# A row scratch with a pitch of 1,280 bytes, in place of a Pool clear between row scatters

## The chip, the cores and the metric

The kernel runs on one core of a Trainium2 chip. The metric is the device time of one execution in microseconds (us), smaller is better; the median of several runs is given with their spread. The engines that matter here are PE (TensorE: matmuls, and PEld, its weight loads), DVE (VectorE), ACT (ScalarE), POOL (GpSimd, which also issues the DMAs of its own queue) and SP (SyncE, which here only issues DMAs). Each engine works through its own instructions in program order and waits on semaphores for the others.

## The reference

Two stages. The first is an attention in which the blocks of k and v are mixed by a Sinkhorn-normalised matrix, with batch 4, 8 heads, 768 positions and head size 64, in 8 blocks of 96 positions. The second is a mixture of 8 experts with one expert per token, on 3,072 tokens of width 512.

```python
for _ in range(5):                      # P: 8 x 8 for each batch and head
    P = np.exp(P - np.max(P, axis=-1, keepdims=True))
    P = P / (np.sum(P, axis=-1, keepdims=True) + 1e-09)
    P = P / (np.sum(P, axis=-2, keepdims=True) + 1e-09)
k_sorted = np.einsum('bhij,bhjcd->bhicd', P, k_b)      # v likewise
attn = softmax(q_b @ k_sorted^T / 8)                   # inside each block of 96
x = (attn @ v_sorted)                                  # 3072 tokens x 512
logits = x @ w_gate + modality_bias[modality_id]
e_idx = np.argmax(logits, axis=1)
gate_w = softmax(logits)[e_idx]
for e in range(8):
    h = np.maximum(x[mask] @ w1[e], 0.0)               # 512 -> 1024
    out[mask] = gate_w[mask, None] * (h @ w2[e])       # 1024 -> 512
```

## The kernel before

**Chunks.** The attention runs in 32 units; unit u is one head of two batches and four blocks. Eight units finish one chunk: 768 tokens in 8 tiles of 96, all 512 columns of them. The four chunks are called m = 0 to 3. A finished chunk lies in SBUF as `xb`, 96 partitions by 8 tiles by 516 bf16 columns: 512 of x, then the token's number and its gate weight as two 32-bit words.

**Routing.** When a chunk is complete, `gate_T` and `gate_L` compute its logits, `choose(m)` takes the expert of each token, and `place(m)` (lines 491 to 544) gives each token a row in a scratch in DRAM. The scratch, `xs_dram` (line 54), has a region of 3,328 rows for each expert, plus 256 rows at its end; a row is 258 32-bit words, 1,032 bytes, and the next row begins right behind it. PE counts ranks into `rk`; DVE turns them into a row number per token: `selr` (L508), `dstf` (L511), and `dest`, the same as integers (L512). The gate weight goes into `xb` at L516, the token's number by a Pool copy at L520. Then `one(t)` (lines 524 to 537) is called for t = 0 to 7: each call sends the 96 rows of one tile to their places with an indirect DMA on Pool's queue (L529). From t = 1 on a `nop` goes before it, and in chunks 1 to 3 also a Pool `memset` of 128 partitions by 512 columns of `kT[0]` (L527), a tile that nothing reads any more by then.

**Slots.** The experts work on slots of 256 rows. `x_fetch` (L650 to L661) reads a slot from the scratch: a DMA transpose (L652) on SP's queue brings x, with its 512 columns on the partitions, into one of four `xT` buffers, and a small DMA (L656) brings the token numbers and gates into `idg`. Of the two experts that get most tokens, `table(m)` (L556) tells after each chunk which slots are full: after chunk 0 slots 0 and 1, after chunk 1 slots 2 and 3, after chunk 2 slots 4 to 7, after chunk 3 slots 8 to 11 and a last half slot 12. The first transpose of each such group waits for all eight scatters of its chunk. `pad_fill` (L622) writes 256 rows of zeros behind the last token of each of the two experts, `zero_block` (L617) does so at the scratch's end; `pair_rows` (L606) is the view of 256 rows that these and L656 use. Whatever is left for other experts is done in a loop at the end, which is empty for this input.

**Experts.** For each slot `mL1` (L681) multiplies with the first weights (4 steps of 8 matmuls into `hp`, L685) and `mL2` (L705) with the second (2 steps of 8 matmuls into `yp`, L708); `y_out` (L689) scales the result by the gate (L695 on ACT or L697 on DVE) and scatters it to the output with an indirect DMA on Pool's queue (L699).

**Order.** The order of the program is written out by hand: the loop over the units (L891 to L903) interleaves scores, softmax and attention of the units with these steps, and from unit 16 on with the experts' steps, one or two for each unit (`pace`, L888). So each engine has one fixed order, in which PE's expert steps of a new group of slots stand among the attention units of the next chunk. Pool's queue holds, one behind the other: the scatters of a chunk with what lies between them, then the output scatters (L699) of the slots that were ready meanwhile, then the token numbers' copy (L520) of the next chunk.

Of the kernel before, what the change touches and what calls it, by code (L numbers as in the profile page):

```python
# [12 lines left out]
ALU = mybir.AluOpType  # L13
# [4 lines left out]
def kernel(  # L18
# [13 lines left out]
    nc = tc.nc  # L32
# [4 lines left out]
    N, Dm = out.shape  # L37
    E = moe_w_gate.shape[1]
    F = moe_w1.shape[2]

    GW = Dm + 4
    NTL = N // BLK
    PR = 256
    CAP = N + PR
    ZR = E * CAP
# [5 lines left out]
    I32 = mybir.dt.int32  # L51
    SYNC = mybir.DependencyInfo(mybir.DependencyClass.Sync, mybir.DependencyReason.DATA)

    xs_dram = nc.dram_tensor("xs_scratch", [ZR + PR, GW // 2], I32, kind="Internal").ap()

    singles = ctx.enter_context(tc.tile_pool(name="singles", bufs=1))
    small = ctx.enter_context(tc.tile_pool(name="small", bufs=1))
# [16 lines left out]
    kT = [singles.tile([128, GC], BF16, tag=f"kT{g}", name=f"kT{g}") for g in range(2)]  # L74
# [4 lines left out]
    attnT = [singles.tile([96, 8 * BLK + 32], BF16, tag=f"attnT{z}", name=f"attnT{z}") for z in range(2)]  # L79
    xb = [singles.tile([BLK, 8, GW], BF16, tag=f"xb{z}", name=f"xb{z}") for z in range(2)]  # L80
    xTg = [singles.tile([128, 8, BLK], BF16, tag=f"xTg{z}", name=f"xTg{z}") for z in range(2)]
# [6 lines left out]
    hT_b = [t.rearrange("p (f r) -> p f r", f=8) for t in (hT_0, qTb[0][:, 4096:6144])]  # L88
    zpad = singles.tile([128, GW], BF16, tag="zpad")

    def q_in(g, hh):
# [8 lines left out]
    nc.sync.dma_start(out=BT[:, 0:2], in_=moe_modality_bias.rearrange("(o m) e -> o m e", o=1).broadcast_to([128, 2, E]))  # L100
    modI = xTg[1].rearrange("p a b -> p (a b)").bitcast(I32)[0:NTL, 0:2 * BLK]
    nc.sync.dma_start(out=modI, in_=bass.AP(tensor=mod_w.tensor, offset=mod_w.offset,
                                            ap=[[2 * BLK, NTL], [1, 2 * BLK]]))
    wg_sb = singles.tile([128, 4, E], FP32)
# [11 lines left out]
    def load_q(g, h0, nh):  # L116
        t = q_in(g, h0 // 4).rearrange("p (r h f) -> p r h f", r=2, h=4)
        z = h0 % 4
        for par in range(2):
            nc.gpsimd.dma_start(out=t[:, par, z:z + nh], in_=q[2 * g + par, h0:h0 + nh]  # L120
                                .rearrange("h (p t) d -> p h (t d)", t=6))
# [8 lines left out]
    pI = singles.tile([128, 1], I32)  # L130
    idI = singles.tile([BLK, NTL], I32)
    load_q(0, 0, 2)
# [9 lines left out]
    nc.gpsimd.iota(pI, pattern=[[0, 1]], base=0, channel_multiplier=1)  # L142
    nc.gpsimd.iota(idI, pattern=[[BLK, NTL]], base=0, channel_multiplier=0)
    nc.gpsimd.iota(jI, pattern=[[1, 2], [0, 2]], base=0, channel_multiplier=0)
# [18 lines left out]
    for e in range(1, E):  # L163
# [7 lines left out]
                     ap=[P_t.ap[0], P_t.ap[2], P_t.ap[1]])  # L171
# [3 lines left out]
                   ap=[ident.ap[0], [1, NB], [NB, 16]])  # L175
# [81 lines left out]
    for it in range(5):  # L257
# [10 lines left out]
        for f in gap[it]:  # L268
# [7 lines left out]
                       ap=[red.ap[0], [0, NB], red.ap[1]])  # L276
# [29 lines left out]

    biasm = singles.tile([BLK, NTL, E], FP32)
    modB = singles.tile([NTL, 6, 16], BF16)
    modF = singles.tile([BLK, NTL], FP32)
# [30 lines left out]
    def use(act=0.0, dve=0.0):  # L340
        busy[0] += act
        busy[1] += dve
# [148 lines left out]
    def place(m):  # L491
        oh, ls = oh_t[m]
        xt = xb[m % 2]
        prev = ohs[m % 2]
        rk = mipsum.tile([128, 8, E], FP32, tag="mi", name=f"rk{m}")
        rkf = rk.rearrange("p t e -> p (t e)")
        pb = bass.AP(tensor=prev.tensor, offset=prev.offset, ap=[prev.ap[0], [0, 8], prev.ap[1]])
        nc.tensor.matmul(rkf, maskUT[0:BLK, :], oh.rearrange("p t e -> p (t e)"), start=True, stop=False,
                         skip_group_check=True)
        nc.tensor.matmul(rkf, ones_bf[0:BLK, :], ebase.rearrange("p t e -> p (t e)"), start=False, stop=False,  # L500
                         skip_group_check=True)
        nc.tensor.matmul(rk, ones_bf[0:BLK, :], pb, start=False, stop=False, skip_group_check=True)
        for t in range(7):
            ob = bass.AP(tensor=oh.tensor, offset=oh[:, t].offset, ap=[oh.ap[0], [0, 7 - t], [1, E]])
            nc.tensor.matmul(rk[:, t + 1:8], ones_bf[0:BLK, :], ob, start=False, stop=(t == 6),
                             skip_group_check=True)
        sel_r = small.tile([BLK, 8, E], FP32, tag="selr", name=f"selr{m}")
        nc.vector.tensor_tensor(sel_r, rk[0:BLK], oh, ALU.mult)  # L508
        dest = small.tile([BLK, 8], I32, tag="dest", name=f"dest{m}")
        dstf = small.tile([BLK, 8], FP32, tag="dstf", name=f"dstf{m}")  # L510
        nc.vector.tensor_reduce(dstf, sel_r, AX.X, ALU.add)  # L511
        nc.vector.tensor_copy(dest, dstf)  # L512
        sm = small.tile([BLK, 8, 1], FP32, tag="sm", name=f"sm{m}")
        nc.vector.tensor_reduce(sm, ls, AX.X, ALU.add)
        gcol = xt.bitcast(FP32)[:, :, Dm // 2 + 1:Dm // 2 + 2]
        nc.vector.reciprocal(gcol, sm)  # L516
        g, hf = m // 2, m % 2
        icol = xt.bitcast(I32)[:, :, Dm // 2]
        idm = idI.rearrange("p (b f j) -> p b f j", b=4, f=2)[:, 2 * g:2 * g + 2, hf]
        nc.gpsimd.tensor_copy(icol.rearrange("p (r j) -> p r j", r=2), idm)  # L520
        scat[m] = []
        use(dve=1.5)

        def one(t):
            if t:
                if m:
                    nc.gpsimd.memset(kT[0][:, 0:512], 0.0)  # L527
                nc.gpsimd.nop()
            ins = nc.gpsimd.indirect_dma_start(  # L529
                out=xs_dram, out_offset=bass.IndirectOffsetOnAxis(ap=dest[:, t:t + 1], axis=0),  # L530
                in_=xt.bitcast(I32)[:, t], in_offset=None)
            after = []
            tc.declare_no_dep(ins.ins, group="xs", reason="rows are disjoint", **({"keep": after} if after else {}))
            tc.add_to_no_dep_group("xs", ins.ins)
            for pre in after:
                tc.add_manual_dep(ins.ins, pre.name, SYNC, reason="rows leave at an even pace")
            scat[m].append(ins.ins)
        ones_[m] = one
        for t in range(8):
            one(t)  # L540
        nxt = ohs[(m + 1) % 2]
        ohsum = small.tile([BLK, E], FP32, tag="ohsum", name=f"ohsum{m}")
        nc.vector.tensor_reduce(ohsum, oh.rearrange("p t e -> p e t"), AX.X, ALU.add)
        nc.vector.tensor_tensor(nxt, ohsum, prev, ALU.add)
# [59 lines left out]
    pads = []  # L604

    def pair_rows(row):  # L606
        return xs_dram[bass.ds(row, PR)].rearrange("(t p) w -> p t w", t=2)

    zsrc = zpad.bitcast(I32)
    zsrc2 = bass.AP(tensor=zsrc.tensor, offset=zsrc.offset, ap=[zsrc.ap[0], [0, 2], zsrc.ap[1]])  # L610

    def in_xs_group(ins, keep=()):
        kw = {"keep": list(keep)} if keep else {}
        tc.declare_no_dep(ins, group="xs", reason="rows are disjoint or ordered by hand", **kw)
        tc.add_to_no_dep_group("xs", ins)

    def zero_block():  # L617
        ins = nc.sync.dma_start(out=xs_dram[ZR:ZR + PR].rearrange("(t p) w -> p t w", t=2), in_=zsrc2)
        in_xs_group(ins.ins)
        pads.append(ins.ins)  # L620

    def pad_fill(e, own=True):  # L622
        row = nc.values_load(prow[0:1, e:e + 1], engines=(SPEng,), min_val=0, max_val=ZR - PR)
        ins = nc.sync.dma_start(out=pair_rows(row), in_=zsrc2)
        if own:
            in_xs_group(ins.ins)
            pads.append(ins.ins)
# [22 lines left out]
    def x_fetch(s, row, own, after=(), n=PR):  # L650
        view = xs_dram[bass.ds(row, n)]
        i1 = nc.sync.dma_start_transpose(out=xT_b[s % NX][:, :, 0:n], in_=view.bitcast(BF16)[:, 0:Dm])  # L652
        xins[s] = i1
        if own:
            nc.sync.nop()
        i2 = nc.sync.dma_start(out=idg_b[s % NI], in_=pair_rows(row)[:, :, Dm // 2:GW // 2])  # L656
        if own:
            for i in (i1, i2):
                in_xs_group(i.ins, after)
                for a in after:  # L660
                    tc.add_manual_dep(i.ins, a.name, SYNC, reason="rows of the slot")  # L661
# [133 lines left out]
    make_upper_triangular(nc, maskUT, val=1.0, diag=False)  # L795
    nc.gpsimd.iota(zpad.bitcast(I32)[:, Dm // 2:Dm // 2 + 1], pattern=[[0, 1]], base=SKIP, channel_multiplier=0)
    zero_block()

    st = {"tab": -1, "x": 0, "l1": 0, "done": 0, "pos": 0}
# [110 lines left out]
    choose(3)  # L910
    run_pieces(2)
    place(3)
    run_pieces(2)
    table_x(3)
# [35 lines left out]
    for s in range(NREST):  # L950
# [3 lines left out]
        row = nc.values_load(tR2[0:1, s:s + 1], engines=(SPEng,), min_val=0, max_val=ZR)  # L954
# [36 lines left out]
```

## Time and profile before

| | |
|---|---|
| median of 3 runs | 214.34 us (212.81, 214.34, 214.37) |
| the profiled execution: its time | 212.81 us |
| its span, first to last instruction | 210.9 us |
| so, around the span | 1.9 us |
| mean clock granted to TensorE | 0.876 of full |
| PE busy | 169.5 us, 80% of the span |
| DVE / ACT / POOL busy | 103.7 / 93.2 / 94.9 us |
| row scatters (L529) | 32 of 0.925 us mean, 29.6 us of POOL |
| clears between them (L527) | 21 of 0.539 us median |
| output scatters (L699) | 25 of 0.982 us mean |
| first to last row scatter of chunks 0, 1, 2, 3 | 54.98 to 64.16, 80.25 to 91.83, 111.68 to 123.07, 142.48 to 153.88 us |

Times are counted from the span's start. A line of the timeline gives the start, the duration, the engine (SPq is SP's queue), the source line and operation, what it writes and reads, how many instructions are merged, and in brackets how long the engine was idle before it and what ended that. In the chain of waits, each line is a start, the time that the step takes on the path that ended last, and what it is. A row of the table of stretches gives a stretch, its length, PE's busy time and number of matmuls in it, the granted clock, the busy share of the 16 DMA engines and the GB/s that they moved.

### The profile page before, as it was taken

Reading aid. Unit: us, or ns where it says so; the run is one execution under the profiler, and the core shown is the slowest. Engines: PE = TensorE matmul, PEld = TensorE weight load, DVE = VectorE, ACT = ScalarE, POOL = GpSimd, SP = SyncE. Lnnn points to the kernel's source line nnn. Section 1 sums busy time; section 2 is a strip of 40 time slices with the busy share of each in tenths; the row PEclk is TensorE's granted clock in tenths of the full one; section 3 lists DMA queues with packets and bytes.
Section 4 is the critical chain, followed back from the end, with each engine's and each line's share of the span. In section 5 each row is a group of like instructions: output and inputs, shape, how many; then the busy total and the mean of one; then the engine's idle time right before and its main releaser. Section 6 shows DMA issues by size and latency. Waiting matters only on the chain.

```text
span 210.9 us, 5167 instructions
## 1 busy us (share of the span) xinstructions
PE 169.5 (80%) x2045; PEld 122.5 (58%) x2045; DVE 103.7 (49%) x333; ACT 93.2 (44%) x148; POOL 94.9 (45%) x139
## 2 busy tenths in 40 slices
PE   6397497769999799995899993999995999999200
PEld 2136496659789686863666753767754667654000
DVE  5968377855787777850355551358221232222100
ACT  2037277836788776853335831334321222232000
POOL 7901378920472027984007983048972232323300
PEclk9859679955699999999559999799999999999955
DMA  4999999999993789729101239536239852212100
GB/s 59 211 225 200 199 223 195 201 181 218 204 242 86 87 131 188 176 82 252 28 0 38 60 106 240 82 83 208 58 105 234 155 99 78 81 71 99 61 2 0
DMA packets 30160, 27.66 MB, mean 131 GB/s; under 512 B 18831, under 2 KB 25775, under 8 KB 29872
## 3 DMA queue, kind: packets, MB, share of 16 engines
q0 software_dynamic: 11792, 23.10, 49.9%
q1 hardware_dynamic: 18336, 4.16, 11.8%
q8 instruction: 18, 0.29, 0.6%
q14 instruction: 14, 0.11, 0.2%
HBM read 27.35 MB, written 10.52 MB: 180 GB/s over the span
## 4 chain that ended last, share of the span: by engine, by line
PE 57%; DVE 10%; POOL 9%; issue 7%; DMA 7%; ACT 4%; POOLq 0%; DVEq 0%; SPq 0%; ACTq 0%
PE hp L685 18%; PE yp L708 16%; DMA xT<-xs_scratch 6%; PE va L375 4%; PE ka L366 3%; PE sc L418 3%; POOL xs_scratch L529 3%; PE gt L450 3%; PE lg L456 3%; DVE xb L441 3%; PE op L437 3%; POOL v_sb L120 2%; PE warm L249 2%; ACT v_sb L353 2%; POOL kT L527 2%
## 5 line engine op out<-in xcount | busy, mean ns | idle before, releaser
L685 PE MATMUL hp<-xT,w 128*128 128x256 bf16 x384 | 51.2, 287 | 8.8 <-DMA xT<-xs_scratch 8.7
L685 PEld LDWEIGHTS <-w 128*128 128x128 bf16 x384 | 37.6, 102 | 18.5 <-DMA xT<-xs_scratch 9.4
L529 POOL DMA_INDIRECT xs_scratch<-xb,dest x32 | 29.6, 925 | 36.6 <-issue 35.3
L699 POOL DMA_INDIRECT out_dram<-kvb,idg x25 | 24.5, 982 | 42.4 <-DVE kvb L697 20.8
L424 ACT ACTIVATE attnT<-sc 96x768 bf16<-96x768 f32 x32 | 25.9, 809 | 13.4 <-PE sc L418 13.0
L708 PE MATMUL yp<-w,hT 128*128 128x512 bf16 x96 | 22.8, 382 | 0.0
L708 PE MATMUL yp<-w,qT 128*128 128x512 bf16 x96 | 22.7, 379 | 0.0
L441 DVE TENSOR_TENSOR xb<-op,rs 96x512 bf16<-96x512 f32 x32 | 22.0, 687 | 1.2
L679 ACT ACTIVATE hT<-hp 128x512 bf16<-128x512 f32 x17 | 10.1, 597 | 22.0 <-PE hp L685 21.8
L697 DVE TENSOR_SCALAR kvb<-yp,idg 128x512 f32<-128x512 f32 x11 | 8.3, 751 | 20.2 <-PE yp L708 20.2
L695 ACT ACTIVATE kvb<-yp,idg 128x512 f32<-128x512 f32 x13 | 8.9, 688 | 17.6 <-PE yp L708 17.6
L679 ACT ACTIVATE qT<-hp 128x512 bf16<-128x512 f32 x16 | 9.6, 597 | 14.7 <-PE hp L685 14.3
L437 PE MATMUL op<-v_sb,attnT 96*128 96x65 bf16 x256 | 14.4, 202 | 0.8 <-DVE xb L441 0.4
L708 PEld LDWEIGHTS <-hT 128*128 128x128 bf16 x96 | 9.1, 99 | 9.3 <-issue 0.3
L708 PEld LDWEIGHTS <-qT 128*128 128x128 bf16 x96 | 9.1, 98 | 9.0
L418 PE MATMUL sc<-qT,kT 64*128 64x96 bf16 (+1 forms) x256 | 12.7, 223 | 1.8 <-ACT attnT L424 0.9
L375 PE MATMUL va<-bd,kvb 128*128 128x128 bf16 x128 | 13.5, 269 | 0.0
L440 DVE RECIPROCAL rs<-op 96x8 f32<-96x8 f32 x32 | 6.4, 199 | 13.7 <-PE op L437 13.7
L437 PEld LDWEIGHTS <-attnT 96*128 96x128 bf16 x256 | 11.8, 103 | 1.9 <-DVE xb L441 0.8
L366 PE MATMUL ka<-bd,kvb 128*64 128x64 bf16 x384 | 9.6, 216 | 4.0 <-issue 2.8
L375 PEld LDWEIGHTS <-kvb 128*128 128x128 bf16 x128 | 12.6, 195 | 0.2
L450 PE MATMUL gt<-ident,xb 96*128 96x96 bf16 x128 | 9.4, 224 | 4.2 <-DVE xb L441 4.1
(180 smaller groups left out, 241.5 us busy)
## 6 DMA issues: line engine op xcount, KB each, us to landing
w<-in_moe_w_dram POOLq DMA_DIRECT2D x4, 1024.0 KB
kvb<-in_k_dram POOLq DMA_DIRECT2D x4, 768.0 KB
kvb<-in_v_dram POOLq DMA_DIRECT2D x2, 1536.0 KB, 17.8
q_in<-in_q_dram POOLq DMA_DIRECT2D x4, 384.0 KB, 16.5
xs_scratch<-zpad SPq DMA_DIRECT2D x3, 258.0 KB
v_sb<-in_q_dram POOLq DMA_DIRECT2D x4, 192.0 KB, 4.0
v_sb<-in_q_dram POOLq DMA_DIRECT2D x2, 384.0 KB, 19.8
xs_scratch<-xb,dest POOLq DMA_INDIRECT x32, 3.3
```

What stands on the lines that cost most here:

```text
L366: nc.tensor.matmul(acc[par * 64:(par + 1) * 64, z], k_raw[:, (c0 + z) * D:(c0 + z + 1) * D], bd[g][:, par * 64:(par + 1) * 64], start=True ...
L375: nc.tensor.matmul(acc[:, z], v_cols[:, d0 + z], bd[g], start=True, stop=True)
L418: nc.tensor.matmul(sc[0:m, par, j * BLK:(j + 1) * BLK], kT[g][rows, x0:x0 + m], qT[rows, i], start=True, stop=True)
L424: mark[0] = nc.scalar.activation(attnT[u % 2][:, 0:8 * BLK].rearrange("p (r f) -> p r f", r=2), sc_tiles.pop(u)[0:BLK, :, 0:4 * BLK], ACT. ...
L437: nc.tensor.matmul(ov[:, par, j], attnT[u % 2][:, c0:c0 + 128], v_sb[g][0:BLK, par * 64 + h * 8 + i, 0:D + 1], start=True, stop=True)
L441: nc.vector.tensor_tensor(xt[:, :, h * D:(h + 1) * D].rearrange("p (r j) d -> p r j d", r=2), ov[0:BLK, :, :, 0:D], rs.broadcast_to([BLK, ...
L450: nc.tensor.transpose(tp[:, t], xb[m % 2][:, t, c * 128:(c + 1) * 128], ident[:BLK, :BLK])
L529: ins = nc.gpsimd.indirect_dma_start(out=xs_dram, out_offset=bass.IndirectOffsetOnAxis(ap=dest[:, t:t + 1], axis=0), in_=xt.bitcast(I32)[: ...
L679: mark[0] = nc.scalar.activation(dst, src, ACT.Relu)
L685: nc.tensor.matmul(hp[:, f], w_at(s, c * F + (2 * j + f) * 128, 128), xT_b[s % NX][:, c], start=(c == 0), stop=(c == 3))
L699: ins = nc.gpsimd.indirect_dma_start(out=out, out_offset=bass.IndirectOffsetOnAxis(ap=idg[:, t, 0:1], axis=0), in_=y, in_offset=None, boun ...
L708: nc.tensor.matmul(yp, hT_b[s % 2][:, fc, t * 128:(t + 1) * 128], w_at(s, 4 * F + fc * Dm, Dm), start=(fc == 0), stop=(fc == 7))
```

## The change

The scratch's rows get a pitch of XP = 5 * 512 / 8 = 320 words, 1,280 bytes (five times 256), of which the first 258 words are used as before. Each row so begins on a multiple of 256 bytes from the scratch's start. The scatter's target is seen as a list of single words, and `dest` holds the word at which the row begins (the row number times 320) in place of the row number. The views that read and fill rows take the first 258 words of each. The `memset` between the scatters of chunks 1 to 3 goes; the `nop` stays.

```diff
     GW = Dm + 4
+    XP = 5 * Dm // 8
...
-    xs_dram = nc.dram_tensor("xs_scratch", [ZR + PR, GW // 2], I32, kind="Internal").ap()
+    xs_dram = nc.dram_tensor("xs_scratch", [ZR + PR, XP], I32, kind="Internal").ap()
...
         nc.vector.tensor_reduce(dstf, sel_r, AX.X, ALU.add)
-        nc.vector.tensor_copy(dest, dstf)
+        nc.vector.tensor_scalar(dest, dstf, float(XP), None, ALU.mult)
...
         def one(t):
             if t:
-                if m:
-                    nc.gpsimd.memset(kT[0][:, 0:512], 0.0)
                 nc.gpsimd.nop()
             ins = nc.gpsimd.indirect_dma_start(
-                out=xs_dram, out_offset=bass.IndirectOffsetOnAxis(ap=dest[:, t:t + 1], axis=0),
+                out=xs_dram.rearrange("r (x o) -> (r x) o", o=1), out_offset=bass.IndirectOffsetOnAxis(ap=dest[:, t:t + 1], axis=0),
                 in_=xt.bitcast(I32)[:, t], in_offset=None)
...
     def pair_rows(row):
-        return xs_dram[bass.ds(row, PR)].rearrange("(t p) w -> p t w", t=2)
+        return xs_dram[bass.ds(row, PR), 0:GW // 2].rearrange("(t p) w -> p t w", t=2)
...
     def zero_block():
-        ins = nc.sync.dma_start(out=xs_dram[ZR:ZR + PR].rearrange("(t p) w -> p t w", t=2), in_=zsrc2)
+        ins = nc.sync.dma_start(out=xs_dram[ZR:ZR + PR, 0:GW // 2].rearrange("(t p) w -> p t w", t=2), in_=zsrc2)
```

## The prediction

> **What bounds the kernel now.** I read the page's slices first, to find where PE isn't full and where its clock is low.
>
> ```profile
> PE   6397497769999799995899993999995999999200
> ...
> PEclk9859679955699999999559999799999999999955
> ```
>
> A slice is 5.27 us. From slice 11 on PE is nearly full except at slices 18, 24 and 30 (about 95, 126 and 158 us), and the granted clock is low at slices 19 and 20 and lower at 25, just behind the first two of these holes. The timeline of PE says what the holes are:
>
> ```profile
> 95.91 0.34 PE L418 MATMUL sc<-qT,kT 64*128 64x96 bf16 x8
> 98.83 1.05 PE L685 MATMUL hp<-xT,w 128*128 128x256 bf16 x8 [2.58 <-DMA xT<-xs_scratch]
> ...
> 126.01 0.48 PE L456 MATMUL lg<-wgp,xTg 128*96 128x8 bf16 x8
> 129.98 1.05 PE L685 MATMUL hp<-xT,w 128*128 128x256 bf16 x8 [3.48 <-DMA xT<-xs_scratch]
> ...
> 156.00 1.89 PE L708 MATMUL yp<-w,hT 128*128 128x512 bf16 x8
> 160.51 1.70 PE L685 MATMUL hp<-xT,w 128*128 128x256 bf16 x14 [2.63 <-DMA xT<-xs_scratch]
> ```
>
> Three stalls, each on the first transposed rows of a group of slots, after chunks 1, 2 and 3: 2.58 + 3.48 + 2.63 = 8.69 us. The chain of waits says what these rows waited for:
>
> ```profile
> 91.83 2.38 DMA xs_scratch<-xb,dest
> 94.40 4.38 DMA xT<-xs_scratch
> 98.83 1.05 PE hp L685 x8
> ```
>
> The last scatter of chunk 1 is issued at 91.83 and lands 2.38 us later; SP then issues the transpose, which lands after 4.38 us. So Pool's row of eight scatters is on the path. Its timeline, the end of chunk 0 (no clears) and of chunk 1:
>
> ```profile
> 60.00 0.92 POOL L529 DMA_INDIRECT xs_scratch<-xb,dest  x1 [0.30 <-issue]
> 61.22 0.92 POOL L529 DMA_INDIRECT xs_scratch<-xb,dest  x1 [0.30 <-issue]
> ...
> 90.20 0.92 POOL L529 DMA_INDIRECT xs_scratch<-xb,dest  x1 [0.17 <-issue]
> 91.11 0.54 POOL L527 MEMSET kT<- 128x512 bf16 x1
> 91.83 0.91 POOL L529 DMA_INDIRECT xs_scratch<-xb,dest  x1 [0.17 <-issue]
> ```
>
> Without a clear a scatter follows the last after 1.22 us (0.92 and 0.30 of issue), with it after 1.63 (0.92, 0.54, 0.17). Last, the clock by stretches:
>
> ```profile
> 98.00:100.00 2.00, 1.18 (x16) 1.00 1.08 322
> 100.00:102.00 2.00, 0.98 (x16) 0.67 0.49 79
> 102.00:104.00 2.00, 2.00 (x16) 0.50 0.00 0
> ...
> 110.00:112.00 2.00, 2.00 (x16) 0.77 0.00 0
> 112.00:114.00 2.00, 2.00 (x24) 1.00 0.18 50
> ```
>
> About 2.5 us after the first stall ended, the clock fell to half for some 10 us, with PE full throughout. After the second it was low from about 132 to 135, after the third not at all.
>
> **The clears.** Chunk 1's scatters span 11.58 us, chunk 2's 11.39, chunk 3's 11.40. Chunk 0 makes six clear-free steps from 54.98 to 62.44, 7.46 us, so seven are 8.70. The last scatter comes earlier by 2.88, 2.69 and 2.70. Nothing hides the clears: Pool is next used by the scatters themselves. The first scatter of a chunk waits for the gate weights and row numbers, so it stays where it is in the order of the work. Behind the eight stand output scatters (L699), which come earlier too; four of them run beside the transpose in chunk 1 (93.05 to 97.91), and may now be done partly before it.
>
> Against the stalls: the first shrinks from 2.58 by 2.88, so it closes with 0.30 us to spare; the second from 3.48 to 0.79; the third from 2.63 by 2.70, closed with 0.07 to spare. Sum 2.58 + 2.69 + 2.63 = 7.90 us. A later stall doesn't give the gain back: each chunk's place step stands in PE's order behind the stall before it, so its scatters move along.
>
> **The clock.** If the low stretches come from the stalls, they go with them. At half clock the eight matmuls of an L1 step at 102.33, 105.06 and 107.32 hold PE for 1.68, 1.83 and 1.68 us; at full clock those at 115.42 and 116.93 take 0.88. That is 5.19 - 2.64 = 2.55 us. The smaller groups between 101 and 112.4 lose 0.1 to 0.4 each against the same groups after 112.4 (transposes 0.75 against 0.34, scores 0.44 against 0.28 three times, logits 0.64 against 0.36, attention 0.54 against 0.35, L2 1.98 against 1.73): 1.6 us more. In the second stretch 16 matmuls take 3.16 in place of 1.75. Sum 2.55 + 1.6 + 1.4 = 5.5 us. PE alone sets the pace there: of 99 to 111 us DVE is busy 5.25 and ACT 4.09. The remaining stall of 0.79 should cost no clock: from 72 to 74 PE was busy 0.97 of 2 us and the clock stayed at 1.00.
>
> A rule speaks against this term. The Trainium skill, "TensorE: Matmul & The Clock Gate", Part 1, says that the array is throttled after about 3.4 us of idleness in a free-running window. By it a stall of 2.58 us needn't have caused the drop, the drop might stay, and only the 7.90 would be won. The trace has the drop after 2.58 us and none after 2.63, so idleness alone isn't its whole cause; I go by the place of the two drops, behind two of three stalls, and by 75 to 95 us, where PE is full and the clock never falls.
>
> **The pitch.** The number of rows, packets and used bytes stays. On DVE a cast of 0.17 to 0.23 us (L512) becomes a multiply with the same shapes; the nearest small multiply, L508, takes 0.22, so at most 0.05 us per chunk, and L516 behind it delays the first scatter by as much: 0.15 us in all, and it may use up the 0.07 of chunk 3. No row of this trace reads or writes aligned rows, so their price is bounded by the spread of rows that there are: a transpose lands in 3.2 us with little beside it (chunk 0) and in 4.4 beside output scatters, a scatter in 2.4 us (chunk 2) and in 4.6 in the median of chunk 0. I take no change, since size and count are what these rows share. A transpose slower by the whole 1.2 costs at most 3.6 over three chunks, less the 0.37 to spare; one faster by as much is worth only the 0.79 that is left, since the other stalls are closed already.
>
> The skill's "DMA: Bandwidth & Descriptors", How a descriptor splits into AXI transactions, says that a piece that begins off a 256-byte boundary pays for one more transaction. No row here shows it; by it the transposes' 256-byte pieces would move faster, the 0.79 would go, and the sum would be less by that.
>
> **Sum.** 7.90 + 5.5 - 0.15 = 13.25. The profiled execution took 212.81 (210.9 of span and 1.9 around it): 199.6. It is the fastest of three by 1.5 us, against the median it would be 201.1; where the others lost 1.5 isn't shown, and a lower clock behind a stall is the likeliest place, which goes. I say 200.0.
>
> **The rivals.** *The stalls go, the low clock stays.* Then 212.81 - 7.90 + 0.15 = 205.1, up to 206.6 against the median. For it: the third stall had no drop behind it, and there was a low stretch from 43 to 56 us that no such stall explains.
>
> *Unpaced scatters land late.* The clears also space the rows out. In chunk 0, which has none, landings took 3.6 to 7.6 us against 2.4 in chunk 2. If the last scatter of each chunk lands 7.6 us after its issue, 5.2 later than now, the path loses 5.2 - 2.8 = 2.4 us per chunk, 7.2 in all: 220, and up to 4 more if the third stall too then costs a low clock as the first did. It decides from the point where the last landing grows by 2.8 us. For it: two loads of 1 MB for the second expert are in the same queue until 87.4 us, and six scatters of chunk 1 would be issued before they end. Against it: chunk 0's landings fall in a stretch in which the DMA engines' share was over 1.2 until 61; in chunks 1 to 3 it is 0.2 to 0.3 once the loads are done, so each scatter uses about a fifth of the time between two, and at 1.22 us still a quarter. Chunk 2 has no loads at all.
>
> *Rows in single words.* The scatter's target is now a list of words. If it is carried out word by word, a scatter is 96 x 258 = 24,768 pieces. The hardware queue's 18,336 packets, most of them 8 to 256 bytes, took 11.8% of 16 engines' 210.9 us, 21.7 ns each; so 33.6 us a scatter, over 1,000 us for 32. The row's source is one run of words, which speaks against it.
>
> *No change.* If the first transpose waits for something else that ends near where the clears let the scatters end, the stalls stay. The number table is written by 86.2 us in chunk 1 and the buffers of its two slots had no earlier user, so I see nothing of the kind.
>
> **How the numbers follow.** Forecast (stalls and low clock go, 197 to 203.5, its ends the 0.79 and some of the 1.5 below, 3.5 of slower transposes above): 0.55. Clock stays (203.5 to 208): 0.19. No change: 0.07. Late landings: 0.15. Single words: 0.04. About 1%, some 2 us, is what a measurement of this kernel can tell from no change. Faster: 0.74, same: 0.07, slower: 0.19. The range takes in the first two cases and some way towards no change: 196.5 to 211; the likeliest case's own is 197 to 203.5.
>
> **What would show it.** In the new profile: scatters of chunks 1 to 3 every 1.22 us, last to first 8.6 to 8.7; the last one's landing at 2.4; PE's idle time before the first L1 step of slots 2, 4 and 8 near 0, 0.8 and 0.1; a granted clock of 1.00 from 57 to the end of the work, a mean near 0.90. Wrong would be: landings beyond 5 us, a new wait ahead of the scatters, or a clock that falls near 100 us with PE full before it.

## The result, and the profile after

| | before | after |
|---|---|---|
| median of 4 runs (lowest, highest) | 213.78 us (212.81, 214.37) | 200.09 us (199.40, 200.92) |
| the profiled execution; its span | 212.81; 210.9 us | 200.92; 199.3 us |
| mean clock granted to TensorE | 0.876 | 0.891 |
| PE / DVE / POOL busy | 169.5 / 103.7 / 94.9 us | 165.7 / 101.6 / 83.5 us |

The ratio after to before is 0.9365, with a 95% interval of 0.9306 to 0.9425: 13.7 us by the medians. The profiled execution of after is the slowest of its four and that of before the fastest of its four, so the two traces differ by only 11.9. A ratio in this document leaves out runs over 1.5% above the fastest of the same kernel, while a median counts every run, so the two can differ a little.

The page's slices of after, now 4.98 us each; PE's busy tenths and the granted clock:

```profile
PE   6397298877999989999899997999999999999000
...
PEclk9859759985556999999999999999999999999955
```

Of the three holes one is left, at slice 24 (about 122 us), and the clock stays full from slice 13 to the end of the work. Slices count from 0. Pool's timeline at the end of chunk 1 (start, duration, engine, line and operation, and the idle time before it):

```profile
89.28 0.91 POOL L528 DMA_INDIRECT xs_scratch<-xb,dest  x1 [0.30 <-DMA xs_scratch<-xb,dest]
90.49 0.91 POOL L528 DMA_INDIRECT xs_scratch<-xb,dest  x1 [0.31 <-issue]
91.70 1.01 POOL L698 DMA_INDIRECT out_dram<-kvb,idg  x1 [0.30 <-DVE lacc L466]
```

A scatter follows the last after 1.21 us. The eight span 8.75, 8.52 and 8.51 us in chunks 1 to 3, and one scatter still takes 0.92 us. PE's timeline at slots 2, 4 and 8:

```profile
97.40 0.34 PE L419 MATMUL sc<-qT,kT 64*128 64x96 bf16 x8
97.67 1.05 PE L684 MATMUL hp<-xT,w 128*128 128x256 bf16 x8
...
120.77 0.48 PE L457 MATMUL lg<-wgp,xTg 128*96 128x8 bf16 x8
122.50 1.05 PE L684 MATMUL hp<-xT,w 128*128 128x256 bf16 x8 [1.25 <-DMA xT<-xs_scratch]
...
148.59 1.91 PE L684 MATMUL hp<-xT,w 128*128 128x256 bf16 x16
```

Slot 2 begins without a wait, slot 4 after 1.25 us, and slot 8 again without one. The chain of waits around slot 4:

```profile
116.78 1.34 PE yp L707 x6
118.12 4.30 DMA xT<-xs_scratch
122.42 0.08 issue
122.50 1.05 PE hp L684 x8
```

The transpose, 4.30 us, is what ends last there. It was as long before, where PE stood 3.48 us:

```profile
125.63 4.30 DMA xT<-xs_scratch
```

What changed is when it is issued: counted from the chunk's first scatter, after 11.03 us (118.12 - 107.09) in place of 13.95 (125.63 - 111.68). And the stretches behind the place of the first stall (a stretch, its length, PE's busy time and matmuls in it, the granted clock, the DMA share, GB/s):

```profile
98.00:100.00 2.00, 0.98 (x16) 1.00 0.95 202
100.00:102.00 2.00, 2.00 (x34) 1.00 0.22 84
102.00:104.00 2.00, 2.00 (x32) 1.00 0.03 8
```

The clock is 1.00 where before it was 0.67 and 0.50.

Where the time went is seen best when the span is cut at the first row scatter of chunks 1, 2 and 3, taken from Pool's timeline. Each of the last three pieces holds one of the three stalls.

| us | to chunk 1 | 1 to 2 (slot 2) | 2 to 3 (slot 4) | 3 to the end (slot 8) | span |
|---|---|---|---|---|---|
| before | 80.25 | 31.43 | 30.80 | 68.42 | 210.9 |
| after | 81.74 | 25.35 | 26.26 | 65.95 | 199.3 |
| gain | -1.49 | 6.08 | 4.54 | 2.47 | 11.6 |
| old pitch, no clears (first experiment) | 81.17 | 25.35 | 26.44 | 66.14 | 199.1 |
| new pitch, clears (second experiment) | 79.40 | 30.82 | 31.73 | 69.95 | 211.9 |

The three later pieces gain 13.1 us. In the first piece, where little but the rows' pitch changed, the profiled execution of after lost 1.49, most likely by the clock: its early stretch of half clock lasted from 43.0 to 63.5 us, before from 42.7 to 56.3.

### The profile page after: what moved, and what is told of

Read it like the earlier page. It is cut to its first block, busy times and chain, and to the rows that moved or that the text cites. A ratio compares the mean times of both kernels' runs of the same rounds, so it can differ in the third digit from the quotient of the medians.

```text
span 199.3 us, 5146 instructions
## 1 busy us (share of the span) xinstructions
PE 165.7 (83%) x2045; PEld 120.8 (61%) x2045; DVE 101.6 (51%) x333; ACT 93.3 (47%) x148; POOL 83.5 (42%) x118
## 3 DMA queue, kind: packets, MB, share of 16 engines
q0 software_dynamic: 11792, 23.10, 52.9%
## 4 chain that ended last, share of the span: by engine, by line
PE 67%; DVE 11%; ACT 5%; issue 4%; POOL 4%; DMA 2%; POOLq 0%; DVEq 0%; ACTq 0%
PE hp L684 20%; PE yp L707 19%; PE va L376 5%; PE sc L419 4%; PE lg L457 3%; PE ka L367 3%; PE op L438 3%; PE gt L451 3%; DVE xb L442 3%; DMA xT<-xs_scratch 2%; POOL v_sb L121 2%; PE warm L250 2%; ACT v_sb L354 2%; ACT attnT L425 2%; PE tq L237 1%
## 5 line engine op out<-in xcount | busy, mean ns | idle before, releaser
L684 PE MATMUL hp<-xT,w 128*128 128x256 bf16 x384 | 47.3, 273 | 1.2 <-DMA xT<-xs_scratch 1.2
L684 PEld LDWEIGHTS <-w 128*128 128x128 bf16 x384 | 36.0, 98 | 9.0 <-DMA xT<-xs_scratch 1.5
L376 PE MATMUL va<-bd,kvb 128*128 128x128 bf16 x128 | 14.0, 281 | 0.0
L438 PEld LDWEIGHTS <-attnT 96*128 96x128 bf16 x256 | 11.9, 104 | 2.1 <-DVE xb L442 0.9
L354 ACT CAST v_sb<-va 96x512 bf16<-96x512 f32 x20 | 11.0, 591 | 3.3 <-PE va L376 2.7
```

The lines of the kernel that those rows point to most:

```text
L376: nc.tensor.matmul(acc[:, z], v_cols[:, d0 + z], bd[g], start=True, stop=True)
L438: nc.tensor.matmul(ov[:, par, j], attnT[u % 2][:, c0:c0 + 128], v_sb[g][0:BLK, par * 64 + h * 8 + i, 0:D + 1], start=True, stop=True)
L684: nc.tensor.matmul(hp[:, f], w_at(s, c * F + (2 * j + f) * 128, 128), xT_b[s % NX][:, c], start=(c == 0), stop=(c == 3))
```

## The experiments

All edits are to the kernel named; each run was compared with the kernel before on the same chip.

**The clears alone: old pitch, no clears.** From the kernel before:

```diff
             if t:
-                if m:
-                    nc.gpsimd.memset(kT[0][:, 0:512], 0.0)
                 nc.gpsimd.nop()
```

> The kernel before with the clears taken out of chunks 1 to 3 and the pitch left at 1,032 bytes. Theory (the clears are the whole gain, the pitch is worth nothing): as the changed kernel, 199 to 201.5 us, scatters every 1.21 to 1.22 us, the last of each chunk landing after 2.4 to 3.6 us. Rival (only aligned rows let unpaced scatters land in time): landings of the last scatter beyond 5 us in chunks 1 to 3 and a time of 206 us or more. Second rival (the pitch has a part of its own): 202 to 206 us with landings as now but transposes that land later than in the changed kernel.

Measured: 199.9 us (198.54 to 200.87), ratio 0.9331 (0.9236 to 0.9425). Its scatters, too, follow each other after 1.21 us. PE's timeline at slot 4:

```profile
122.11 1.05 PE L683 MATMUL hp<-xT,w 128*128 128x256 bf16 x8 [1.43 <-DMA xT<-xs_scratch]
```

Spacing, remaining stall and the three later pieces in the table above are those of after within 0.2 us; the first piece is 0.57 shorter. Leaving the clears out is enough for the whole gain, as far as these runs can tell.

**The pitch alone: new pitch, with the clears.** From the kernel after:

```diff
             if t:
+                if m:
+                    nc.gpsimd.memset(kT[0][:, 0:512], 0.0)
                 nc.gpsimd.nop()
```

> The changed kernel with the clears put back: pitch of 1,280 bytes alone. Theory: as the kernel before, 212.5 to 215 us, with three stalls of about 2.6, 3.5 and 2.6 us and the half clock behind the first. Rival (the pitch speeds up the transposes or scatters by itself): stalls shorter by 0.5 us or more each, 208 to 211 us.

Measured: 214.99 us (210.83 to 216.15, ten runs) against 214.03, ratio 0.9938 (0.9863 to 1.0012). PE's timeline shows all three stalls again:

```profile
98.23 1.05 PE L686 MATMUL hp<-xT,w 128*128 128x256 bf16 x8 [2.83 <-DMA xT<-xs_scratch]
...
128.48 1.89 PE L686 MATMUL hp<-xT,w 128*128 128x256 bf16 x8 [3.44 <-DMA xT<-xs_scratch]
...
160.24 2.66 PE L686 MATMUL hp<-xT,w 128*128 128x256 bf16 x16 [2.88 <-DMA xT<-xs_scratch]
```

2.83, 3.44 and 2.88 us, against 2.58, 3.48 and 2.63, and the clock is halved behind each of them, for 6.8, 6.8 and 3.4 us. The interval takes in no change, so the pitch has no effect on the time that can be told. It does have one on the DMA engines. The hardware queue, which carries the transposes among other loads, has the same packets in all four kernels (number, MB, share of 16 engines' span). Its line on the page, with the old pitch, in before and then in the first experiment:

```profile
q1 hardware_dynamic: 18336, 4.16, 11.8%
```

```profile
q1 hardware_dynamic: 18336, 4.16, 13.9%
```

and with the new pitch, in this experiment and then in after:

```profile
q1 hardware_dynamic: 18336, 4.16, 10.4%
```

```profile
q1 hardware_dynamic: 18336, 4.16, 11.2%
```

Times the spans, that is 24.9 and 27.7 us of all 16 engines with the old pitch, 22.0 and 22.3 with the new: 11% less with the clears, 19% less without them. The other traces agree on the sign, less on the size: 25.0 us in the one with the old pitch, 22.2 to 23.4 in the seven with the new.

**One chunk's clears at a time.** From the kernel after, with the condition `m == 1`, `m == 3` and `m == 2`:

```diff
             if t:
+                if m == 1:
+                    nc.gpsimd.memset(kT[0][:, 0:512], 0.0)
                 nc.gpsimd.nop()
```

> The changed kernel with the clears put back in chunk 1 alone. Theory (the low clock is caused by the stall): a stall of 2.4 to 2.9 us before the first L1 step of slot 2, then half clock for some 10 us, which costs about 4 more: 206 to 208 us. Rival (the low clock has nothing to do with the stall): the stall alone, 202.5 to 203.5 us, and a clock of 1.00 behind it.

Measured: 204.73 us (203.50 to 205.68), ratio 0.9565 (0.9473 to 0.9657). PE's timeline at slot 2, and the stretches behind it:

```profile
97.23 0.34 PE L419 MATMUL sc<-qT,kT 64*128 64x96 bf16 x8
100.19 1.53 PE L686 MATMUL hp<-xT,w 128*128 128x256 bf16 x8 [2.61 <-DMA xT<-xs_scratch]
```

```profile
98.00:100.00 2.00, 0.00 (x0) 1.00 1.03 316
100.00:102.00 2.00, 1.81 (x16) 0.65 1.00 247
102.00:104.00 2.00, 0.98 (x15) 0.50 0.27 43
104.00:106.00 2.00, 2.00 (x16) 0.50 0.00 0
```

The stall is back, and the clock halves from 100.6 to 107.4 us. That stretch is 6.8 us long; before it had been 10.2. From the first L1 step of slot 2 to chunk 2's first scatter it takes 11.82 us here and 12.85 before, so the shorter stretch accounts for about 1 us of what the time came out below the 206 to 208 expected.

> The changed kernel with the clears put back in chunk 3 alone. Theory: a stall of 2.4 to 2.8 us before the first L1 step of slot 8; if the clock holds as it did behind this stall in the kernel before, 202.3 to 203.3 us. Rival (a stall of that length costs the clock wherever it is): some 10 us of half clock in dense expert matmuls, 5 us more, 207 to 208.5 us.

Measured: 203.53 us (201.07 to 204.80), ratio 0.9461 (0.9336 to 0.9585). PE's timeline at slot 8 and one later line of the same 16 matmuls:

```profile
150.04 3.57 PE L686 MATMUL hp<-xT,w 128*128 128x256 bf16 x16 [3.13 <-DMA xT<-xs_scratch]
...
155.17 1.91 PE L686 MATMUL hp<-xT,w 128*128 128x256 bf16 x16
```

A stall of 3.13 us, and now the half clock follows the third stall too: 3.57 against 1.91 us, from 150.0 to 153.4. So the missing drop behind the third stall before was no property of that place. The time lies between the two that were expected, as the drop lasted 3.4 us and not 10.

> The changed kernel with the clears put back in chunk 2 alone. Theory (the three chunks' clears add up to the whole gain of 13.7 us; chunk 1's gave 4.6, chunk 3's 3.4): 2.7 us of stall on top of the 1.25 that is left at slot 4, and a low clock behind it of 3.4 to 10 us: 204.5 to 206.5 us. Rival (the gains overlap, so that one alone costs less than its share): under 203.5 us.

Measured: 229.82 us, ratio 1.0242 (1.0139 to 1.0346), on a chip on which the kernel before itself took 224.1. PE's timeline of it:

```profile
65.03 0.80 PE L457 MATMUL lg<-wgp,xTg 128*96 128x8 bf16 x8 [6.79 <-issue]
```

PE stands still for 6.79 us with no releaser shown, and other engines stand still at the same times, also well before chunk 2. This run says nothing of chunk 2, and the same kernel was run again on another chip, beside the kernel after:

> The changed kernel itself once more, beside the next one on the same chip. On a chip on which the kernel before takes 213 to 215 us: 199 to 201.5 us. On the chip of the last run, where it took 224.1: if the clears cost there what they cost elsewhere, 210 to 211; if idle times of other kinds hide them there, 215 us or more.

> The changed kernel with the clears put back in chunk 2 alone, a second time, since the kernel before took 224.1 us on the chip of the first. Theory (the chunks' clears add up): 4.5 to 6.5 us over the changed kernel on the same chip. Rival (one chunk's clears alone cost less than its share): under 3.5 us over it.

Measured: the kernel after 199.12 us (198.64 to 201.26), ratio 0.9300 (0.9212 to 0.9389); with chunk 2's clears 204.24 (203.08 to 205.14), ratio 0.9499 (0.9416 to 0.9583). PE's timeline of the latter at slot 4:

```profile
124.45 1.33 PE L686 MATMUL hp<-xT,w 128*128 128x256 bf16 x8 [3.52 <-DMA xT<-xs_scratch]
```

The stall is 3.52 us, and the clock is halved from 125.1 to 128.5. Against the kernel without clears that ran on the same chip (for chunks 1 and 3 the first experiment, with the old pitch), chunk 1's clears cost 4.8 us (204.73 - 199.90), chunk 3's 3.6 (203.53 - 199.90) and chunk 2's 5.1 (204.24 - 199.12). They sum to 13.5, and all three together are worth 13.7: each chunk pays for itself. The medians are of runs that spread by 2 to 4 us, but the trace with chunk 1's clears shows too that nothing is given back later: its two later pieces take 26.25 and 65.24 us, those of after 26.26 and 65.95.

**The stalls without the low clock.** From the kernel before, matmuls on constants into the `hp` of slots 2, 4 and 8, ahead of its first real step; the waits stay, but PE is busy in them:

```diff
+        if j == 0 and s in (2, 4, 8):
+            for z in range({2: 10, 4: 14, 8: 10}[s]):
+                nc.tensor.matmul(hp.rearrange("p f r -> p (f r)"), ones_bf, wsrc, start=True, stop=True)
```

> The kernel before, clears and old pitch, with 10, 14 and 10 extra matmuls of 512 columns on constants in front of the first L1 step of slots 2, 4 and 8; their results are overwritten. They fill the three stalls (0.216 us each at full clock) and should leave the rows' arrival as it is. Theory (part of the gain was the clock): the same three waits for the rows measured from the last real matmul, 2.6 to 3.5 us, but a clock of 1.00 behind them, and 207.5 to 210 us. Rival (the low clock costs nothing, DVE or ACT set the pace there): 212.5 to 215 us with the clock at 1.00.

Measured: 210.26 us (208.00 to 211.61), ratio 0.9842 (0.9797 to 0.9886). PE's timeline at slot 2 and the stretches behind it:

```profile
96.35 2.33 PE L685 MATMUL hp<-ones_bf 128*128 128x512 bf16 x10
99.19 1.03 PE L688 MATMUL hp<-xT,w 128*128 128x256 bf16 x8 [0.51 <-DMA xT<-xs_scratch]
```

```profile
100.00:102.00 2.00, 0.98 (x23) 1.00 0.91 136
102.00:104.00 2.00, 2.00 (x36) 1.00 0.04 8
```

Slot 2 still waits for its rows, but the clock stays at 1.00, there and behind slots 4 and 8. So it is PE's idleness in these stalls that lowers the clock behind them, and without the low clock the kernel gains 3.9 us by the medians (214.15 - 210.26), 3.4 by the ratio (2.4 to 4.3). The time is just outside the range that my theory gave, on its upper side, and well below the rival's, in which the low clock costs nothing. The gain would be larger if the rows had not come later in this run: from a chunk's first scatter to the first L1 step of its slots the trace takes 18.77, 18.85 and 18.17 us, before 18.58, 18.30 and 18.03. Why they came later stays open.

**Clears of twice the size.** From the kernel after:

```diff
+                if m:
+                    nc.gpsimd.memset(kT[0][:, 0:1024], 0.0)
```

> The changed kernel with clears of 1,024 columns, twice the old length, in chunks 1 to 3. Theory (Pool's row of scatters is the path of each chunk): a scatter every 2.15 us, the last one of a chunk 3.7 us later than with the old clears, three stalls of 6.3 to 7.2 us, 225 us and 0 to 8 more for the clock. Rival (something else than Pool's row sets the stalls): less than 3 us more per chunk, under 222 us.

Measured: 224.66 us (223.66 to 225.79), ratio 1.0496 (1.0428 to 1.0565). A clear takes 0.96 us and scatters follow each other after 2.05. The time is the one expected, the stalls only in part (6.3 to 7.2 each): slots 4 and 8 wait 6.17 and 6.41 us, but slot 2 only 2.20, because PE had already lost 1.84 ahead of it and then ran at half clock from 90.4 to 93.8. The timeline of PE, of the same kernel, names what held it up there:

```profile
90.42 0.82 PE L451 MATMUL gt<-ident,xb 96*128 96x96 bf16 x8 [1.84 <-DVE xb L442]
```

and DVE's shows why `xb` was late:

```profile
86.00 1.54 DVE L578 TENSOR_SCALAR tb_ti<-tb_ti 1x8 int32<-1x8 int32 x1
...
87.77 0.15 DVE L580 TENSOR_TENSOR tb_a<-tb_f,dd 1x2 f32<-1x2 f32 x1
...
88.32 1.27 DVE L584 TENSOR_SCALAR tabR<-tb_r 1x2 int32<-1x2 f32 x1
```

Operations on one partition and a few numbers take 1.54 and 1.27 us, and both end (at 87.54 and 89.59) where one of Pool's clears ends. Pool's timeline there:

```profile
86.55 0.97 POOL L528 MEMSET kT<- 128x1024 bf16 x1
...
88.61 0.96 POOL L528 MEMSET kT<- 128x1024 bf16 x1
```

This led back to the same lines of the kernel before, on DVE's timeline in chunk 2:

```profile
115.54 0.28 DVE L577 TENSOR_SCALAR tb_ti<-tb_ti 1x8 int32<-1x8 int32 x1
115.86 0.56 DVE L578 CAST tb_f<-tb_ti 1x8 f32<-1x8 int32 x1
...
117.05 0.40 DVE L583 TENSOR_SCALAR tabR<-tb_r 1x4 int32<-1x4 f32 x1
```

and of the kernel after:

```profile
110.67 0.16 DVE L576 TENSOR_SCALAR tb_ti<-tb_ti 1x8 int32<-1x8 int32 x1
110.86 0.16 DVE L577 CAST tb_f<-tb_ti 1x8 f32<-1x8 int32 x1
...
111.61 0.16 DVE L582 TENSOR_SCALAR tabR<-tb_r 1x4 int32<-1x4 f32 x1
```

0.28, 0.56 and 0.40 us have become 0.16 each.

**An attempt to go further.** The low clock from 43 us on is left in the kernel after. Two dummy matmuls after each of units 2 to 8 and six dummy transposes ahead of chunk 0's gate were to keep it up:

```diff
+        if m == 0:
+            for t in range(6):
+                nc.tensor.transpose(tp[:, t], ident[:BLK, :], ident[:BLK, :BLK])
...
+        if 2 <= u < 9:
+            fill = mipsum.tile([128, 512], FP32, tag="mi", name=f"fill{u}")
+            for z in range(2):
+                nc.tensor.matmul(fill[:, 0:256], ones_bf, wsrc[:, 0:2], start=True, stop=True)
```

> The changed kernel with extra PE work on constants in the first chunk's gaps: two matmuls of 256 columns after each of units 2 to 8, and six transposes ahead of each of chunk 0's four groups of transposes; results unused or overwritten. Theory (the low clock from 43 to 56 or 63 us comes from PE's many short waits there, about a quarter of the time): the clock stays at 1.00 from 30 us on and the time is 194 to 198 us. Rival (the low stretch isn't caused by PE's own load): it stays, and the fill costs 0 to 2 us: 200 to 202 us.

Measured: 200.7 us (199.67 to 203.88), ratio 0.9371 (0.9340 to 0.9402): no gain over after that can be told, so the time that the theory gave did not come. The stretches and, after them, Pool's timeline at the last scatter of chunk 0:

```profile
50.00:52.00 2.00, 1.56 (x55) 1.00 1.15 222
52.00:54.00 2.00, 0.84 (x32) 0.69 1.23 200
54.00:56.00 2.00, 1.96 (x37) 0.50 1.32 203
```

```profile
63.75 0.95 POOL L531 DMA_INDIRECT xs_scratch<-xb,dest  x1 [2.93 <-DMA w<-in_moe_w_dram]
```

The low clock only began later, at 52.7 us. The first seven scatters of chunk 0 came 2.6 us sooner (59.90 against 62.47 for the seventh), but the eighth then waited 2.93 us for the weight loads, and the first transpose was issued at 66.22 against 66.86. There the loads set the pace. The piece up to chunk 1 still ended 1.41 us sooner than in the profiled execution of after (80.33 us), but slots 2 and 4 then waited 0.27 and 2.38 us, in place of 0 and 1.25. Behind the 2.38 the clock stayed at 1.00.

## Why the prediction was right

**The clears.** Pool's row of scatters was on the path, as the steps said: spacing 1.21 us (1.22 foretold), the eight in 8.5 to 8.75 (8.6 to 8.7). The three single-chunk runs show that each chunk's gain holds without the others.

**The stalls.** 7.90 us of PE's idle time were to go; 8.69 - 1.25 = 7.44 went. Idle time is not the best measure, though. The traces, cut also at the first L1 step of slots 2, 4 and 8, show better what was won where (each piece begins where the one before it ends):

| us | chunk 1's first scatter to slot 2 | to chunk 2's | to slot 4 | to chunk 3's | to slot 8 | to the end |
|---|---|---|---|---|---|---|
| before | 18.58 | 12.85 | 18.30 | 12.50 | 18.03 | 50.39 |
| after | 15.93 | 9.42 | 15.41 | 10.85 | 15.24 | 50.71 |
| gain | 2.65 | 3.43 | 2.89 | 1.65 | 2.79 | -0.32 |
| stalls kept, PE busy in them | 18.77 | 9.40 | 18.85 | 10.83 | 18.17 | 49.76 |

From a chunk's first scatter to the first step of its slots 2.65, 2.89 and 2.79 us were won, 8.33 in all. Slot 4 kept 1.25 us of idle time where 0.79 was foretold, though its row of scatters is 2.87 us shorter (2.69 foretold) and its transpose takes 4.30 us as before. The reason is that PE came there sooner: its own way from the chunk's first scatter, the stall left out, is 14.16 us (15.41 - 1.25) in place of 14.82 (18.30 - 3.48). Slots 2 and 8 closed, with little to spare: in the second execution of after on another chip slot 2 waited 0.59 and slot 4 1.36.

**Landings.** The 2.4 us of the last scatter held in chunks 2 and 3 (the transposes are issued 2.51 and 2.77 us after the last scatter). In chunk 1 it became 3.56, before 2.57; the first experiment, with the old pitch, has 3.52 there, and the second, with the clears, 2.58. So closer scatters can meet the second expert's loads, as the rival *unpaced scatters land late* said, but by 1 us where it needed 2.8, and not always: the run with the dummy matmuls has 2.58 too. Pool's timeline of the second execution of after names the loads:

```profile
86.14 0.91 POOL L528 DMA_INDIRECT xs_scratch<-xb,dest  x1 [0.30 <-issue]
88.62 0.90 POOL L528 DMA_INDIRECT xs_scratch<-xb,dest  x1 [1.57 <-DMA w<-in_moe_w_dram]
```

**The clock.** That the low stretches behind the stalls come from them was right, and the rival *the stalls go, the low clock stays* fell: with the waits kept and PE busy the drops went, and each stall that was put back brought one back. The size was nearly right. Between the first L1 step of slots 2 and 4 and the next chunk's first scatter the trace of after wins 3.43 and 1.65 us, 5.08 in all, where 5.5 were foretold. The trace with the stalls kept has the same 9.40 and 10.83 us there, with the clears in it, so these 5.08 are the clock's. Its own time shows less of it, because its rows came later. The prediction's working put 4.15 us on the first stretch, as if every bit of time that PE lost between 99 and 112 us were on the path, and 1.4 on the second; it also read PE as full throughout the first, in which PE stood 1.02 us up to 101.14, and the clock fell 1.9 us after the stall's end (at 100.7), not 2.5. For the rule on 3.4 us of idleness that the prediction weighed ("TensorE: Matmul & The Clock Gate", Part 1, of the Trainium skill): a wait of 1.84 us (with the doubled clears) and stalls of 2.61, 2.83, 2.88 and 3.13 were each followed by a drop here, one of 2.63 (before, slot 8) was not, nor were 2.38 (with the dummy matmuls) and 1.25. So a stall shorter than that can be enough, its length alone does not decide, and the low stretch behind it, of 3.4, 6.8 or 10.2 us in these runs, can't be sized from the stall: 2.58 us gave the longest, 3.52 one of the shortest.

**DVE.** The step counted 0.15 us of loss for the multiply and nothing else. The multiply costs nothing that can be told (a median of 0.169 us, the cast 0.168). What it missed is that the clears slowed DVE. The operations that write `tb_ti`, `tb_f` and `tabR` (L577, L578 and L583 before) hold DVE 2.1 us less in all, by their groups' means, and DVE's busy time went from 103.7 to 101.6. Little of it reached the time. Before, in chunk 2, the chain of waits ran through them, and from `lacc` (L462) to the next `xb` (L441) passed 2.31 us, after 1.77. But that lies ahead of slot 4's stall, where PE comes 0.66 us sooner now and waits that much longer for its rows. In chunks 1 and 3 PE's own way to slots 2 and 8 became 0.07 and 0.16 us shorter (16.00 to 15.93, 15.40 to 15.24), so 0.2 us is what DVE can have given there.

So the steps measure 8.33 + 5.08 = 13.41 us where 7.90 + 5.5 - 0.15 = 13.25 were foretold; the traces' three later pieces, with the 0.32 lost at the end, give 13.1, the medians 13.7, the ratio's interval 12.3 to 14.8. The mechanism was right in both steps. That two errors of 0.4 us went opposite ways, and that 200.09 was met to 0.1 us where single runs spread by 1.5, is luck.

**The pitch.** No change was taken, and none can be told from the times. The bound of 1.2 us per transpose was wide: the share of the hardware queue fell by 3 to 5 us of 16 engines in all, 0.2 to 0.4 us for each of 13 transposes if it is all theirs; over all traces it is 1.5 to 5.7 us. The skill's rule on pieces that begin off a 256-byte boundary ("DMA: Bandwidth & Descriptors", How a descriptor splits into AXI transactions) points the same way. The prediction took it to close slot 4's stall, and 1.25 us stayed, against 1.43 with the old pitch. *Rows in single words* fell with the scatter's unchanged 0.92 us and the software queue's 11,792 packets, as many as before, *no change* with the result itself.

**The early part.** A clock of 1.00 from 57 us on and a mean near 0.90 were foretold; the profiled execution held the low clock until 63.5, with a mean of 0.891. In three other traces of kernels without clears it ended at 62.7 (the old pitch), 63.0 (dummy matmuls) and 54.3 (the second execution of after). Why it varies stays open.

## What to carry to other kernels

A small instruction on an engine that is half idle can be worth far more than its own time: 21 clears of 0.54 us, 11.3 us of POOL's time, cost 13.7 us, because each stood in the row of work that released the busiest engine, and because most of the stalls of 2 to 4 us there halved the matmul clock for 3 to 10 us after. Where a wait stands behind a delay, shortening the delay only makes the wait longer: that is what became of most of what PE won from the faster DVE. When a change has two parts, run each alone before giving the gain to the one that gave the change its name: here the pitch did nothing to the time that can be told. And where a stall can't be removed, cheap matmuls on constants that fill it won 1.6% (0.9842).

## What the runs showed of the hardware that was not expected

Pool's clears stretch some DVE operations, and not others. In the means by group, the `TENSOR_SCALAR` and the cast of 1 x 8 numbers take 343 and 363 ns before and 170 and 159 after; with the new pitch and the clears they take 414 and 362, without clears and with the old pitch 167 and 159, so it is the clears. With clears of 1,024 columns one such operation took 1.54 us, while the `TENSOR_TENSOR` operations between them, beside a scatter, stayed at 0.15. In chunk 3 of before a clear runs from 145.04 to 145.58: the `SCALAR_TENSOR_TENSOR` at 145.08 takes 0.15 us beside it, the `TENSOR_SCALAR` at 145.26 takes 0.34 and ends with it. But `TENSOR_SCALAR` operations that read the matmuls' results in `hp` take 0.69 us with clears and without. The Trainium skill, "SBUF — State Buffer", section "SBUF: two separate sides", says that VectorE and GpSimd share a pair of ports, that the one that starts first has it for a whole instruction while the other waits, and that this concerns only some of VectorE's operations. That agrees with some growing and some not. It doesn't explain all: the operation of 1.54 us began 0.55 us ahead of the clear that it ended with, beside a scatter, and those of 0.28 and 0.40 us in chunk 2 of before ended just ahead of a clear (at 115.86 and 117.49). The runs show that it is the clears; how they hold DVE is not shown.

One chip ran the kernel before in 224.1 us where others took 213.8 to 214.8, with stretches in which several engines stood still at once and no releaser is shown. What holds them there can't be told from these traces; a comparison on such a chip was of no use for differences of 5 us.
